# Top-k attention and a tanh-shrink feed-forward on one core: one buffer for turned attention weights, and combined feed-forward weights kept in SBUF

## The chip, the core and the metric

The kernel runs on one NeuronCore of a Trainium2 chip. A core has five engines that run their own instruction queues in order and meet through semaphores: TensorE (PE; its weight loads are listed as PEld), VectorE (DVE), ScalarE (ACT), GpSimd (POOL) and SyncE (SP), which here issues nearly all DMAs. Operands lie in SBUF, matmul results in PSUM, inputs and outputs in HBM. The metric is device time in microseconds of the one core, as the median of the timed runs. Beside these there is one profiled execution, whose trace has every instruction.

## The reference

Attention over 8 batches, 8 heads, 576 tokens and a head size of 64, in which each query keeps its 32 largest scores, and then a feed-forward block over all 4608 tokens of 512 values (8 heads of 64), with 2048 inner values:

```python
scores = scale * np.matmul(q, k.transpose(0, 1, 3, 2))
kth = np.partition(scores, -top_k, axis=-1)[..., -top_k:-top_k + 1]
scores = np.where(scores >= kth, scores, -1000000000.0)
attn = np.exp(scores - np.max(scores, axis=-1, keepdims=True))
attn = attn / (np.sum(attn, axis=-1, keepdims=True) + 1e-09)
x = np.matmul(attn, v)          # heads side by side: 4608 x 512
h = x @ w_in                    # 512 x 2048
g = h - np.tanh(h)
out = g @ w_out                 # 2048 x 512
```

`w_in` and `w_out` arrive as float64 and are turned into float32 on the chip.

## The kernel before

**Attention steps.** Work is cut into 144 steps. A step is one block of 128 queries for a pair of heads (`hp`, four pairs per batch); the 64 remaining queries of a batch form a step of their own for two pairs together (a remainder step, `rem`). A batch from 1 on has 18 steps in two parts: in part 0 the query blocks 0 and 1 of all four pairs, in part 1 blocks 2 and 3, with the remainder steps in part 1 (in part 0 for the last batch). Two steps of the same pair in a part make a group: their turned weights lie side by side and are multiplied with the values at once. The 18 steps of batch 0 turn their weights with matmuls on PE (`pe`).

A step n passes through a row of stages, in successive turns of the main loop in `run`: `scores` (PE, copied by ACT at L338), `search` (DVE finds the 32 largest by `max` and `match_replace`), `mask` (POOL sets the thresholds `tb` at L397, ACT and POOL make `z`), `expo` (ACT), `divide` (ACT, L459), `turn_z` (DVE transposes 32x32 blocks into the single buffer `zx`, L491), `spread_keys` (SP writes `zx` to the DRAM tensor `there`, L507, and one turn later brings it back as the turned weights, L510, four DMAs), and five turns after the step `values` (PE, L558, ten pairs of matmuls for a group). `spread_keys` puts the main groups in turn into two places, `et2[0]` (a tile of its own) and `et2[1]` (the front of `later`, a tile that holds raw weights at the start); remainder steps use a third place, `et_rem`.

**Values.** `load_v` brings a batch's values of a head pair, 2 DMAs of 128 KB, once for each part, into three rotating buffers, and in part 0 the remainder rows too (2 small DMAs).

**Feed-forward.** A full unit is 256 tokens; there are 17 of these (and two of 128 tokens, of batch 0). A full unit has 30 items. Sixteen `ffn_h` items multiply with `w_in` (L609), and every second one makes `g` (tanh and copy on ACT, subtraction on POOL, L623). Then 14 `ffn_p` items multiply with `w_out` by Strassen's scheme in Winograd's form: seven products instead of eight, each in two halves k, with the parts of `g` as A11 to A22 and those of `w_out` as B11 to B22. An item is 8 matmuls of 128x256 (L723). The products are

```python
ORDER = [("A11", "B11"), ("A12", "B21"), ("S2", "T2"), ("S3", "T3"), ("S1", "T1"), ("A22", "T4"), ("S4", "B22")]
```

with S1 = A21 + A22, S2 = S1 - A11, S3 = A21 - A11, S4 = A12 - S2 (`sum_up`, POOL, L695) and T1 = B12 - B11, T2 = B22 - T1, T3 = B12 - B22, T4 = B21 - T2, the combinations of the weights. Those are made once, after the start, by `combine` on POOL (16 instructions, one per item). In the kernel before, T1 replaces B12 and T2 replaces B21 in SBUF; B21, T3 and T4 lie in DRAM (`kept`) and are streamed to SBUF for every unit. `stream` does so on SP (L703): six transfers of 512 KB per unit into two places (`flow`, in the tile `more`), one per half k. Products 1, 3 and 5 use these places one after the other, so the next stream into a place waits until the product that reads it is done. `ffn_p` also evicts the results (ACT, L748 to L765), joins them (POOL, L736) and writes the output (L768).

**Order.** The program's order is fixed by hand. In each turn n of `run` the stages are emitted in a set order, and between them `deal` emits feed-forward items from the list `work`: 0.4 of the turn's share after `search`, and 0.2 at three later places. `rate` sets the share so that the list lasts to the end and units come in time. Each engine then has its instructions in this order, and SP its DMAs: a DMA at the head of SP's queue that waits for a semaphore holds those behind it. What is left in `work` after the last turn is emitted at the end. `due` emits the value matmuls; up to turn 45 it comes first in the turn, from 45 on (`NEAR`) after the second half of the scatter (`coming_back`). At the end the kernel looks whether a step's search was too narrow; only then it runs again with an exact search.

Of the kernel before, what the change touches and what calls it, by code (L numbers as in the profile page):

```python
# [19 lines left out]
J = 4  # L20
# [34 lines left out]
def kernel(  # L55
# [59 lines left out]
    def next_h(name):  # L115
# [16 lines left out]
    zx1 = consts.tile([P, 4 * S], FP32, name="zx")[:]  # L132
    et2 = [consts.tile([P, 4 * S], FP32, name="et")[:], later[:, 0 : 4 * S]]
    et_rem = later[:, 4 * S : 6 * S]

    more = consts.tile([P, 4096], FP32, name="more")[:]
    sums = [
        [more[:, (2 * i + k) * 512 : (2 * i + k + 1) * 512].rearrange("p (m n) -> p m n", n=P) for i in range(2)]
        for k in range(2)
    ]  # L140
    flow = [
        more[:, (2 + k) * 1024 : (3 + k) * 1024].rearrange("p (m n) -> p m n", n=2 * P) for k in range(2)
    ]
    qT0 = [more[:, i * S : (i + 1) * S] for i in range(4)]
# [3 lines left out]
    q_first = more[:, 3264 : 3264 + S]  # L148
    temps = [later[:, i * 512 : (i + 1) * 512].rearrange("p (m n) -> p m n", m=2) for i in range(4)]
    kept = {  # L150
        x: keep.tile([P, CF // 2, 2 * P], FP32, name=f"kept{x}") for x in ("B12", "B21", "T3", "T4")
    }

# [111 lines left out]

    def load_v(b, hp, part):


        if b == 0 and hp == NHP - 1:
            x = vb3  # L270
        else:
            x = kqpool.tile([P, 2, J, D], FP32, tag="vb", name="vb", bufs=3)[:]
        vb[b, hp, part] = x
        y = vrs[hp]
        for t in range(2):
            h, o = 2 * hp + t, t * R
            nc.sync.dma_start(
                x[:, t, :, :], v[b, h, o : o + JP, :].rearrange("(c p) d -> p c d", p=P)
            )
            o = 0 if t else JP  # L280
            if part == 0:
                nc.sync.dma_start(y[half(t), t, :], v[b, h, o : o + R, :])

# [191 lines left out]

    zxs, ets, last_et = {}, {}, [1]

# [18 lines left out]
    def spread_keys(n):  # L496


        zx = zxs.pop(n)
        rem = steps[n].rem  # L500
        if not rem:
            last_et[0] ^= 1
        et = ets[n] = et_rem if rem else et2[last_et[0]]
        assert rem or not last_et[0] or combined[0] == 4 * WJ
        w = steps[n].nq * S // 2
        there = dpool.tile([P, NG * w], FP32, tag=f"there{steps[n].nq}", name="there")
        nc.sync.dma_start(there[:], zx[:, 0 : NG * w])  # L507
        yield
        for c in range(NG):
            nc.sync.dma_start(  # L510
                et[group(c), 0 : NG * w].rearrange("i (a x) -> i a x", a=NG),
                there[:, c * w : (c + 1) * w].rearrange("(a i) x -> i a x", a=NG),
            )

    def turn_pe(n):

        g, z = steps[n], st.pop(n)["z"]
        if g.rem:
            et = et_rem
        elif g.i:  # L520
            et = ets.pop(n - 1)
        else:
            et = et2[0]
        ets[n] = et
        et = tiles(et, g.nq)[:, :, :, g.i, :].rearrange("p a k j -> p k a j")
        for k0 in range(0, KC, J):
            kn = min(J, KC - k0)
            zt = zt_ps.tile([P, 512], FP32, tag="zt", name="zt")
            for k in range(kn):
                nc.tensor.transpose(  # L530
                    zt[:, k * P : (k + 1) * P], z[:, (k0 + k) * P : (k0 + k + 1) * P], ident[:]
                )
            nc.scalar.copy(
                et[:, k0 : k0 + kn],
                zt[:, 0 : kn * P].rearrange("p (k a j) -> p k a j", a=NG, j=G),
            )
            if k0:
                yield
# [5 lines left out]
    def values(n):  # L544
# [7 lines left out]
        for i in range(2 if g.rem else 1):  # L552
# [3 lines left out]
            for c in range(J + 1):  # L556
                for t in range(2):
                    nc.tensor.matmul(  # L558
                        av[half(t), 0, cols],
                        vb[g.b, hp, g.part][:, t, c, :] if c < J else vrs[hp][:, t, :],  # L560
                        es[:, :, (J + 1) * t + c if c < J else J].rearrange("p a i j -> p a (i j)"),
                        start=(c == 0),
                        stop=(c == J),
                    )
# [84 lines left out]

    def keep_corners(j):  # L650

        (_, b12), (b21, _) = corners(w_out[j][:])
        nc.sync.dma_start(kept["B12"][:, 2 * j : 2 * j + 2, :], b12)
        nc.sync.dma_start(kept["B21"][:, 2 * j : 2 * j + 2, :], b21)

    def bring_corners():

        for j in range(WJ):
            (_, b12), (b21, _) = corners(w_out[j][:])
            nc.sync.dma_start(b12, kept["B12"][:, 2 * j : 2 * j + 2, :])  # L660
            nc.sync.dma_start(b21, kept["B21"][:, 2 * j : 2 * j + 2, :])

    def combine(j, x):

        (b11, b12), (b21, b22) = corners(w_out[j][:])
        t3, t2, t4 = (temps[(3 * j + i) % 4] for i in range(3))
        ms = slice(2 * j, 2 * j + 2)
        if x == 0:
            nc.gpsimd.tensor_tensor(t3, b12, b22, ALU.subtract)
            nc.sync.dma_start(kept["T3"][:, ms, :], t3)  # L670
        elif x == 1:
            nc.gpsimd.tensor_tensor(b12, b12, b11, ALU.subtract)
        elif x == 2:
            nc.gpsimd.tensor_tensor(t2, b22, b12, ALU.subtract)
        else:
            nc.gpsimd.tensor_tensor(t4, b21, t2, ALU.subtract)
            nc.sync.dma_start(kept["T4"][:, ms, :], t4)
            nc.sync.dma_start(b21, t2)

# [5 lines left out]
    def sum_up(u, k, x):  # L685

        (a11, a12), (a21, a22) = quarters(u, k)
        s1, s2 = sums[k]
        out_, a, b, op = [
            (s1, a21, a22, ALU.add),  # L690
            (s2, s1, a11, ALU.subtract),
            (a21, a21, a11, ALU.subtract),
            (a12, a12, s2, ALU.subtract),
        ][x]
        nc.gpsimd.tensor_tensor(out_, a, b, op)  # L695

    ORDER = [("A11", "B11"), ("A12", "B21"), ("S2", "T2"), ("S3", "T3"), ("S1", "T1"), ("A22", "T4"), ("S4", "B22")]
    FLOW = ["B21", "T3", "T4"]

    def stream(i):  # L700

        x, k = FLOW[i // 2], i % 2
        nc.sync.dma_start(flow[k], kept[x][:, 4 * k : 4 * k + 4, :])  # L703

    def product(u, i, k):
# [6 lines left out]
        (a11, a12), (a21, a22) = quarters(u, k)  # L712
        lhs = {"A11": a11, "A12": a12, "A22": a22, "S1": sums[k][0], "S2": sums[k][1], "S3": a21, "S4": a12}[left]
        acc = cur[u][i % 2][:, 0 : 2 * P]
        fresh = i in (0, 1, 3)
        for m in range(4):
            if right in FLOW:
                rhs = flow[k][:, m, :]
            else:
                r, c = {"B11": (0, 0), "T1": (0, 1), "T2": (1, 0), "B22": (1, 1)}[right]  # L720
                f = 2 * (4 * k + m) + r
                rhs = w_out[f // FJ][:, f % FJ, c * 2 * P : (c + 1) * 2 * P]
            nc.tensor.matmul(acc, lhs[:, m, :], rhs, start=(fresh and k == 0 and m == 0), stop=(k == 1 and m == 3), skip_group_check=True)  # L723
        return acc

    def ffn_p(u, item):
# [10 lines left out]

        if item in (3, 4):
            sum_up(u, item - 3, 3)
        if item < 3:  # L740
            sum_up(u, 1, item)
        if ORDER[i][1] in FLOW[:-1]:
            stream(2 * FLOW.index(ORDER[i][1]) + 2 + k)
        if not k:
# [24 lines left out]

    combined = [0]  # L770

    def combine_next():

        if combined[0] < 4 * WJ:
            combine(combined[0] // 4, combined[0] % 4)
            combined[0] += 1

    def ffn_small_o(u, part):

        ffn_o(u, 0, part)  # L780
        if u.combines and part:
            combine_next()

    def ffn_full(u, item):

        ffn_h(u, item)
        if item in (6, 7):
            stream(item - 6)
        combine_next()
        if 8 <= item < 11:  # L790
            sum_up(u, 0, item - 8)

# [58 lines left out]
    def run(exact):  # L851
        plan()
        turned_pe[0] = not exact
        combined[0], last_et[0] = 0, 1
        if exact:
# [14 lines left out]
        for n, b, hp, part in sorted(rows):  # L870
            for x, name in enumerate("kq"):
# [12 lines left out]
                else:  # L884
                    at(n - 3 + x, turn)
                    turned[name] = n - 3 + x
            at(n + 3 if b else n - 1, lambda b=b, hp=hp, part=part: load_v(b, hp, part))

# [15 lines left out]
        def part(x, k):  # L904
            next(loaded[k][0])
            if x == 2:
                converted[0] = k + 1
                if k >= WJ * CD and k % CD == CD - 1:
                    keep_corners(k // CD - WJ)
                free.append(loaded[k][1])  # L910
# [74 lines left out]
        for n in range(-4, NS + LAG):  # L985
# [6 lines left out]
            if n < NEAR:  # L992
                due()
            share, usable = rate(), converted[0]
            if pe:
# [9 lines left out]
            if pe:  # L1005
                spread(n - 2)
            deal(0.0 if pe else 0.4)
            for x in coming_back:
                next(x, None)
            coming_back.clear()  # L1010
            if n >= NEAR:
                due()
            if here(1):
# [63 lines left out]
```

## Time and profile before

| | |
|---|---|
| timed runs, us | 1591.86, 1593.54, 1600.24 (median 1593.54) |
| the profiled execution's own time, us | 1588.93 |
| its span, first to last instruction, us | 1587.1 |
| mean granted clock of TensorE | 0.962 |
| DMA traffic on SP's queue | 285.83 MB |
| streams of 512 KB (`more` from `kept`) | 102 |
| scatters of main groups (4 x 288 KB) | 56 |
| value loads of 128 KB into the rotating buffers | 118 |

The page first has each engine's busy time and its share of the span. Other views list groups of instructions by line, operation and tile (count, busy time, mean duration, and the idle time just before them with what ended it); the waits (who waited for what, total, times, longest); busy time by stretch with the granted clock of TensorE; and the timeline, in which a line has start, duration, engine, line of the kernel, operation, tiles (out<-in), count, and in brackets the idle time before it. SPq is SP's queue of DMA issues. `more<-keptT` is a stream of T3 or T4, `more<-keptB` one of B21; `hx` and `hy` are the two PSUM banks of the products; a product that reads a streamed operand is in the row `hy<-more,g`. A wait is put down to the last semaphore seen, so a row can name an engine where a DMA was the cause.

### The profile page before, as it was taken

How to read it: one execution, taken by the hardware profiler on the slowest of the kernel's cores; microseconds unless marked ns; L12 is line 12 of the kernel's file. 1: busy time of each engine (PE TensorE's matmuls, PEld its weight loads, DVE VectorE, ACT ScalarE, POOL GpSimd, SP SyncE). 2: the span in 40 equal slices, each digit the busy share in tenths (PEclk: the TensorE clock that was granted, in tenths of full speed). 3: DMA queues.
4: the chain of work that ended last, by engine and by line, in shares of the span. 5: the costliest groups of instructions: out<-in, count | busy, mean ns of one | idle time of the engine just before them, and what ended most of it. 6: DMA issues, size and time to landing. Idle time of an engine off the chain costs nothing.

```text
span 1587.1 us, 27014 instructions
## 1 busy us (share of the span) xinstructions
PE 1410.6 (89%) x7892; PEld 1069.5 (67%) x7892; DVE 1298.0 (82%) x4914; ACT 1017.1 (64%) x1898; POOL 1105.1 (70%) x1573
## 2 busy tenths in 40 slices
PE   4676997898997989898999899989998988989998
PEld 2464755676665667676777677767676766768887
DVE  7998898998999999898989888989988887873000
ACT  4766766766676767676667666767776665664321
POOL 3777799768585767767587767777777674856523
PEclk9778998999999999999999999999999999999999
DMA  9955126777867977778678886778768776673532
GB/s 262 347 186 195 23 74 172 208 197 192 206 172 200 200 202 195 192 175 216 179 189 201 202 205 180 196 194 202 194 181 207 183 166 174 181 201 112 133 93 69
DMA packets 299292, 287.87 MB, mean 181 GB/s; under 512 B 224384, under 2 KB 234624, under 8 KB 291968
## 3 DMA queue, kind: packets, MB, share of 16 engines
q1 hardware_dynamic: 297360, 285.83, 68.4%
q8 instruction: 65, 1.06, 0.3%
q14 instruction: 91, 0.75, 0.2%
q10 hardware_dynamic: 1776, 0.22, 0.1%
HBM read 196.98 MB, written 87.95 MB: 180 GB/s over the span
## 4 chain that ended last, share of the span: by engine, by line
PE 29%; DVE 26%; DMA 13%; ACT 12%; POOL 12%; issue 5%; SPq 3%; DVEq 0%; ACTq 0%; POOLq 0%
PE hps L609 10%; PE hx L723 6%; PE hy L723 6%; DMA more<-keptT 5%; DVE m L379 4%; DMA there<-zx 4%; DVE top L372 4%; POOL g L623 3%; PE av L558 3%; ACT z L459 3%; ACT z L410 3%; PE scps L330 3%; POOL z L413 3%; DVE zx L491 3%; DVE rest L382 2%
## 5 line engine op out<-in xcount | busy, mean ns | idle before, releaser
L609 PE MATMUL hps<-xT,w_in 128*128 128x256 f32 (+1 forms) x2176 | 478.0, 376 | 13.0 <-ACT g L622 12.0
L413 POOL TENSOR_TENSOR z<-sc,z 128x576 f32<-128x576 f32 x288 | 404.6, 1427 | 79.3 <-ACT z L410 79.3
L609 PEld LDWEIGHTS hps<-xT,w_in 128*128 128x128 f32 x2176 | 394.9, 194 | 93.2 <-issue 23.6
L410 ACT ACTIVATE z<-sc,tb 128x576 f32<-128x576 f32 x288 | 207.6, 768 | 245.1 <-POOL tb L397 241.2
L491 DVE STREAM_TRANSPOSE zx<-z 128x1152 f32<-128x1152 f32 x126 | 172.4, 1368 | 107.8 <-ACT z L459 69.2
L623 POOL TENSOR_TENSOR g<-g,th 128x512 f32<-128x512 f32 x144 | 183.4, 1275 | 97.5 <-ACT g L622 96.7
L723 PE MATMUL hy<-more,g 128*128 128x256 f32 x816 | 208.1, 407 | 37.7 <-DMA more<-keptT 35.2
L433 ACT ACTIVATE z<-z,nb 128x576 f32<-128x576 f32 x288 | 221.8, 776 | 2.4 <-POOL z L413 2.4
L459 ACT ACTIVATE z<-z,rd 128x576 f32<-128x576 f32 x252 | 180.4, 763 | 56.7 <-DVE rd L452 56.5
L723 PEld LDWEIGHTS hy<-more,g 128*128 128x128 f32 x816 | 161.2, 202 | 78.4 <-DMA more<-keptT 20.3
L372 DVE MAX8 top<-ab 128x8 f32<-128x144 f32 x864 | 194.5, 293 | 0.0
L330 PE MATMUL scps<-kT,qT 64*128 64x288 f32 (+1 forms) x1120 | 158.3, 430 | 36.1 <-DVE top L368 34.0
L338 ACT COPY sc<-scps 128x1152 f32<-128x1152 f32 x144 | 160.7, 1116 | 35.8 <-PE scps L330 35.8
L379 DVE MAX8 m<-rest 128x8 f32<-128x168 f32 x576 | 161.1, 321 | 0.0
L443 POOL TENSOR_SCALAR rd<-den 128x2 f32<-128x2 f32 x144 | 32.8, 228 | 182.1 <-ACT z L433 177.8
L379 DVE MAX8 m<-top 128x8 f32<-128x144 f32 (+1 forms) x576 | 151.2, 304 | 0.0
L330 PEld LDWEIGHTS scps<-kT,qT 64*128 64x128 f32 (+1 forms) x1120 | 87.3, 177 | 91.0 <-issue 39.3
L723 PE MATMUL hx<-w_out,g 128*128 128x256 f32 x544 | 133.4, 393 | 16.9 <-POOL g L623 10.0
L723 PEld LDWEIGHTS hx<-w_out,g 128*128 128x128 f32 x544 | 102.9, 194 | 44.2 <-POOL g L623 17.6
L723 PE MATMUL hx<-w_out,more 128*128 128x256 f32 x544 | 127.8, 385 | 0.0
L621 ACT ACTIVATE th<-hps 128x512 f32<-128x512 f32 x144 | 84.4, 586 | 55.3 <-PE hps L609 52.8
L723 PEld LDWEIGHTS hx<-w_out,more 128*128 128x128 f32 x544 | 102.6, 191 | 21.1 <-issue 4.7
(107 smaller groups left out, 2220.5 us busy)
## 6 DMA issues: line engine op xcount, KB each, us to landing
there<-zx SPq DMA_DIRECT2D x56, 1152.0 KB, 5.0
more<-keptT SPq DMA_DIRECT2D x68, 512.0 KB, 5.0
et<-there SPq DMA_DIRECT2D x112, 288.0 KB, 5.6
spare<-there SPq DMA_DIRECT2D x112, 288.0 KB, 6.4
more<-keptB SPq DMA_DIRECT2D x34, 512.0 KB, 6.6
vb<-in_v_dram SPq DMA_DIRECT2D x118, 128.0 KB, 5.3
kin<-in_k_dram SPq DMA_DIRECT2D x116, 72.0 KB, 4.2
out_dram<-ot SPq DMA_DIRECT2D x32, 256.0 KB, 2.3
```

What stands on the lines that cost most here:

```text
L330: nc.tensor.matmul(ps[rows, t, s, 0:S2], qT[g.b, g.hp + i, g.part][half(t), qs], kT[g.b, g.hp + i][half(t), ks], start=True, stop=True,)
L338: nc.scalar.copy(sc[:], ps[:, :, :, 0:S2])
L372: nc.vector.max(top[:, t, o : o + 8], low[:, t, i, :])
L379: nc.vector.max(m[:, t, m8], seen[i][t])
L410: nc.scalar.activation(zv[:, t, :], scf[:, t, :], AF.Relu, bias=tb[:, t : t + 1], scale=-BIG)
L413: nc.gpsimd.tensor_tensor(zv[:, t, :], scf[:, t, :], zv[:, t, :], ALU.subtract)
L433: nc.scalar.activation(x["zv"][:, t, :], x["zv"][:, t, :], AF.Exp, bias=x["nb"][:, t : t + 1], scale=scale, accum_out=den[:, t : t + 1],)
L459: nc.scalar.activation(x, x, AF.Copy, scale=rds[n][:, g.i, t : t + 1])
L491: nc.vector.transpose(tiles(zx, g.nq)[:, :, :, g.i, :].rearrange("p c k j -> p k c j"), z[:].rearrange("p (k c j) -> p k c j", c=NG, j=G),)
L609: nc.tensor.matmul(cur[u][:, s : s + w], w_in[j][:, c, fo : fo + P], u.xT[:, c, 0:w], start=(c == 0), stop=(c == CD - 1),)
L623: nc.gpsimd.tensor_tensor(g, g, th[:], ALU.subtract)
L723: nc.tensor.matmul(acc, lhs[:, m, :], rhs, start=(fresh and k == 0 and m == 0), stop=(k == 1 and m == 3), skip_group_check=True)
```

## The change

Five things are different.

Turned weights: main groups after batch 0 all go to one place, `et_main` (the front of `later`). `et_pe`, the former first place, is used in batch 0 and afterwards holds half of T2 and the sum S1. The `due` of turns from 45 on stands ahead of `coming_back`, so that the value matmuls which read the place precede the scatter which writes it.

Weight combinations: B21 stays where it was in `w_out`. T3 has two places in `more`, T4 has two, T2 has two, of which one (T2's half 0 and T4's half 1) is the same memory. These two halves are also in DRAM, and `bring` fetches them in turn: T4's half at item 4 of a unit's products, T2's half at item 11. `keep_corner` saves only B12 (for the exact run).

Combinations have a new order, and a gate: T3 not before turn 17, T2 and T4 not before turn 20, since their places hold other data until then. The first item of the second small unit may now make one too.

Values: `load_v` runs once per batch and pair; the fourth pair has a place of its own (`vb_last`).

Sums: S2 is written over A11 instead of into a place of its own, so it is made after the A11 product of its half: S1 and S3 of half 0 during `ffn_full`, then S1 of half 1 at item 0, S2 of half 0 and S3 of half 1 at item 1, S2 of half 1 at item 2, S4 at items 3 and 4.

```diff
@@ -130,26 +130,26 @@
     zx1 = consts.tile([P, 4 * S], FP32, name="zx")[:]
-    et2 = [consts.tile([P, 4 * S], FP32, name="et")[:], later[:, 0 : 4 * S]]
+    et_pe, et_main = consts.tile([P, 4 * S], FP32, name="et")[:], later[:, 0 : 4 * S]
     et_rem = later[:, 4 * S : 6 * S]
     more = consts.tile([P, 4096], FP32, name="more")[:]
-    sums = [
-        [more[:, (2 * i + k) * 512 : (2 * i + k + 1) * 512].rearrange("p (m n) -> p m n", n=P) for i in range(2)]
-        for k in range(2)
-    ]
-    flow = [
-        more[:, (2 + k) * 1024 : (3 + k) * 1024].rearrange("p (m n) -> p m n", n=2 * P) for k in range(2)
-    ]
+    whole = {
+        "T3": [more[:, 1024 * i : 1024 * (i + 1)] for i in range(2)],
+        "T4": [more[:, 2048:3072], more[:, 3072:4096]],
+        "T2": [more[:, 3072:4096], et_pe[:, 0:1024]],
+    }
+    whole = {x: [y.rearrange("p (m n) -> p m n", n=2 * P) for y in ys] for x, ys in whole.items()}
+    sums = [et_pe[:, 1024 + 512 * i : 1536 + 512 * i].rearrange("p (m n) -> p m n", n=P) for i in range(2)]
     qT0 = [more[:, i * S : (i + 1) * S] for i in range(4)]
...
     q_first = more[:, 3264 : 3264 + S]
-    temps = [later[:, i * 512 : (i + 1) * 512].rearrange("p (m n) -> p m n", m=2) for i in range(4)]
-    kept = {
-        x: keep.tile([P, CF // 2, 2 * P], FP32, name=f"kept{x}") for x in ("B12", "B21", "T3", "T4")
-    }
+    temps = [later[:, i * 512 : (i + 1) * 512].rearrange("p (m n) -> p m n", m=2) for i in range(2)]
+    vb_last = later[:, 6 * S : 6 * S + 512].rearrange("p (t c d) -> p t c d", t=2, d=D)
+    kept_B12 = keep.tile([P, CF // 2, 2 * P], FP32, name="kept_B12")
+    kept = {x: keep.tile([P, 4, 2 * P], FP32, name=f"kept_{x}") for x in ("T2", "T4")}
     e896 = consts.tile([P, 1], FP32, name="e896")
@@ -263,14 +263,14 @@
             o += r1 - r0
-    def load_v(b, hp, part):
-        if b == 0 and hp == NHP - 1:
-            x = vb3
+    def load_v(b, hp):
+        if hp == NHP - 1:
+            x = vb_last if b else vb3
         else:
             x = kqpool.tile([P, 2, J, D], FP32, tag="vb", name="vb", bufs=3)[:]
-        vb[b, hp, part] = x
+        vb[b, hp] = x
         y = vrs[hp]
@@ -278,8 +278,7 @@
             o = 0 if t else JP
-            if part == 0:
-                nc.sync.dma_start(y[half(t), t, :], v[b, h, o : o + R, :])
+            nc.sync.dma_start(y[half(t), t, :], v[b, h, o : o + R, :])
     turned_pe = [True]
@@ -473,7 +472,7 @@
             )
-    zxs, ets, last_et = {}, {}, [1]
+    zxs, ets = {}, {}
     def group(a):
@@ -498,14 +497,12 @@
         rem = steps[n].rem
-        if not rem:
-            last_et[0] ^= 1
-        et = ets[n] = et_rem if rem else et2[last_et[0]]
-        assert rem or not last_et[0] or combined[0] == 4 * WJ
+        et = ets[n] = et_rem if rem else et_main
         w = steps[n].nq * S // 2
...
         yield
+        assert combined[0] >= 12
         for c in range(NG):
@@ -520,7 +517,7 @@
         else:
-            et = et2[0]
+            et = et_pe
         ets[n] = et
@@ -557,7 +554,7 @@
                         av[half(t), 0, cols],
-                        vb[g.b, hp, g.part][:, t, c, :] if c < J else vrs[hp][:, t, :],
+                        vb[g.b, hp][:, t, c, :] if c < J else vrs[hp][:, t, :],
                         es[:, :, (J + 1) * t + c if c < J else J].rearrange("p a i j -> p a (i j)"),
@@ -647,35 +644,36 @@
         return [[x[:, :, r, c * 2 * P : (c + 1) * 2 * P] for c in range(2)] for r in range(2)]
-    def keep_corners(j):
-        (_, b12), (b21, _) = corners(w_out[j][:])
-        nc.sync.dma_start(kept["B12"][:, 2 * j : 2 * j + 2, :], b12)
-        nc.sync.dma_start(kept["B21"][:, 2 * j : 2 * j + 2, :], b21)
+    def keep_corner(j):
+        nc.sync.dma_start(kept_B12[:, 2 * j : 2 * j + 2, :], corners(w_out[j][:])[0][1])
     def bring_corners():
         for j in range(WJ):
-            (_, b12), (b21, _) = corners(w_out[j][:])
-            nc.sync.dma_start(b12, kept["B12"][:, 2 * j : 2 * j + 2, :])
-            nc.sync.dma_start(b21, kept["B21"][:, 2 * j : 2 * j + 2, :])
-    def combine(j, x):
+            nc.sync.dma_start(corners(w_out[j][:])[0][1], kept_B12[:, 2 * j : 2 * j + 2, :])
+    def combine(x, j):
         (b11, b12), (b21, b22) = corners(w_out[j][:])
-        t3, t2, t4 = (temps[(3 * j + i) % 4] for i in range(3))
-        ms = slice(2 * j, 2 * j + 2)
-        if x == 0:
-            nc.gpsimd.tensor_tensor(t3, b12, b22, ALU.subtract)
-            nc.sync.dma_start(kept["T3"][:, ms, :], t3)
-        elif x == 1:
+        k, ms = j // 2, slice(2 * (j % 2), 2 * (j % 2) + 2)
+        t2 = whole["T2"][k][:, ms, :]
+        if x == "T3":
+            nc.gpsimd.tensor_tensor(whole["T3"][k][:, ms, :], b12, b22, ALU.subtract)
+        elif x == "T1":
             nc.gpsimd.tensor_tensor(b12, b12, b11, ALU.subtract)
-        elif x == 2:
+        elif x == "T2":
             nc.gpsimd.tensor_tensor(t2, b22, b12, ALU.subtract)
+            if k == 0:
+                nc.sync.dma_start(kept["T2"][:, ms, :], t2)
         else:
+            t4 = temps[j % 2] if k else whole["T4"][k][:, ms, :]
             nc.gpsimd.tensor_tensor(t4, b21, t2, ALU.subtract)
-            nc.sync.dma_start(kept["T4"][:, ms, :], t4)
-            nc.sync.dma_start(b21, t2)
+            if k:
+                nc.sync.dma_start(kept["T4"][:, ms, :], t4)
+    COMBINE = [("T3", j) for j in range(WJ)] + [("T1", j) for j in range(WJ)]
+    COMBINE += [(x, j) for j in (2, 3, 0, 1) for x in ("T2", "T4")]
     def quarters(u, k):
@@ -685,22 +683,20 @@
         (a11, a12), (a21, a22) = quarters(u, k)
-        s1, s2 = sums[k]
-        out_, a, b, op = [
-            (s1, a21, a22, ALU.add),
-            (s2, s1, a11, ALU.subtract),
-            (a21, a21, a11, ALU.subtract),
-            (a12, a12, s2, ALU.subtract),
-        ][x]
+        s1 = sums[k]
+        out_, a, b, op = {
+            "S1": (s1, a21, a22, ALU.add),
+            "S3": (a21, a21, a11, ALU.subtract),
+            "S2": (a11, s1, a11, ALU.subtract),
+            "S4": (a12, a12, a11, ALU.subtract),
+        }[x]
         nc.gpsimd.tensor_tensor(out_, a, b, op)
     ORDER = [("A11", "B11"), ("A12", "B21"), ("S2", "T2"), ("S3", "T3"), ("S1", "T1"), ("A22", "T4"), ("S4", "B22")]
-    FLOW = ["B21", "T3", "T4"]
-    def stream(i):
-        x, k = FLOW[i // 2], i % 2
-        nc.sync.dma_start(flow[k], kept[x][:, 4 * k : 4 * k + 4, :])
+    def bring(x):
+        k = 0 if x == "T2" else 1
+        nc.sync.dma_start(whole[x][k], kept[x][:])
     def product(u, i, k):
@@ -710,19 +706,27 @@
         (a11, a12), (a21, a22) = quarters(u, k)
-        lhs = {"A11": a11, "A12": a12, "A22": a22, "S1": sums[k][0], "S2": sums[k][1], "S3": a21, "S4": a12}[left]
+        lhs = {"A11": a11, "A12": a12, "A22": a22, "S1": sums[k], "S2": a11, "S3": a21, "S4": a12}[left]
         acc = cur[u][i % 2][:, 0 : 2 * P]
...
         for m in range(4):
-            if right in FLOW:
-                rhs = flow[k][:, m, :]
+            if right in whole:
+                rhs = whole[right][k][:, m, :]
             else:
-                r, c = {"B11": (0, 0), "T1": (0, 1), "T2": (1, 0), "B22": (1, 1)}[right]
+                r, c = {"B11": (0, 0), "T1": (0, 1), "B21": (1, 0), "B22": (1, 1)}[right]
                 f = 2 * (4 * k + m) + r
...
         return acc
+    SUMS = {
+        0: [(1, "S1")],
+        1: [(0, "S2"), (1, "S3")],
+        2: [(1, "S2")],
+        3: [(0, "S4")],
+        4: [(1, "S4")],
+    }
     def ffn_p(u, item):
@@ -735,12 +739,12 @@
             nc.gpsimd.tensor_tensor(a, a, b, ALU.add)
-        if item in (3, 4):
-            sum_up(u, item - 3, 3)
-        if item < 3:
-            sum_up(u, 1, item)
-        if ORDER[i][1] in FLOW[:-1]:
-            stream(2 * FLOW.index(ORDER[i][1]) + 2 + k)
+        for x in SUMS.get(item, []):
+            sum_up(u, *x)
+        if item == 4:
+            bring("T4")
+        if item == 11:
+            bring("T2")
         if not k:
@@ -767,28 +771,29 @@
                     nc.sync.dma_start(dst, x[rows, :])
-    combined = [0]
+    combined, now = [0], [0]
     def combine_next():
-        if combined[0] < 4 * WJ:
-            combine(combined[0] // 4, combined[0] % 4)
+        if combined[0] < len(COMBINE):
+            x, j = COMBINE[combined[0]]
+            if now[0] < (17 if x == "T3" else 20 if x in ("T2", "T4") else 0):
+                return
+            combine(x, j)
             combined[0] += 1
...
         ffn_o(u, 0, part)
-        if u.combines and part:
+        if u.combines:
             combine_next()
...
         ffn_h(u, item)
-        if item in (6, 7):
-            stream(item - 6)
         combine_next()
-        if 8 <= item < 11:
-            sum_up(u, 0, item - 8)
+        if item in (8, 9):
+            sum_up(u, 0, ("S1", "S3")[item - 8])
     def ffn(u):
@@ -851,7 +856,7 @@
         turned_pe[0] = not exact
-        combined[0], last_et[0] = 0, 1
+        combined[0] = 0
         if exact:
@@ -884,7 +889,8 @@
                     turned[name] = n - 3 + x
-            at(n + 3 if b else n - 1, lambda b=b, hp=hp, part=part: load_v(b, hp, part))
+            if not part:
+                at(n + 3 if b else n - 1, lambda b=b, hp=hp: load_v(b, hp))
@@ -906,7 +912,7 @@
                 if k >= WJ * CD and k % CD == CD - 1:
-                    keep_corners(k // CD - WJ)
+                    keep_corner(k // CD - WJ)
                 free.append(loaded[k][1])
@@ -991,7 +997,7 @@
                 due()
-            share, usable = rate(), converted[0]
+            share, usable, now[0] = rate(), converted[0], n
             if pe:
@@ -1005,11 +1011,11 @@
             deal(0.0 if pe else 0.4)
+            if n >= NEAR:
+                due()
             for x in coming_back:
...
             coming_back.clear()
-            if n >= NEAR:
-                due()
             if here(1):
```

## The prediction

> **What bounds the kernel now.** I read the page's engine sums first, then the busy time by stretch, the waits, and the timeline around one long wait.
>
> ```profile
> span 1587.1 us, 27014 instructions
> PE 1410.6 (89%) x7892; PEld 1069.5 (67%) x7892; DVE 1298.0 (82%) x4914; ACT 1017.1 (64%) x1898; POOL 1105.1 (70%) x1573
> ...
> 250.00:1440.00 1190.00, 1085.88 (x6109) 822.76 (x6109) 1062.62 (x4072) 808.36 (x1500) 859.30 (x1247) 0.97 0.76 192
> 1440.00:1587.10 147.10, 139.74 (x676) 118.25 (x672) 13.14 (x40) 39.79 (x82) 64.71 (x67) 0.99 0.36 105
> ```
>
> The columns of the last two lines are the stretch, its length, busy us of PE, weight loads, DVE, ACT and POOL, the granted clock, DMA share and GB/s. The run has three stages. Up to 250 us weights are converted. From 250 to 1440 the attention steps run with the feed-forward work dealt in between: PE is busy 91% and DVE 89%, so no engine alone is the bound. They hold each other up through in-order queues. From 1440 to the end PE works off what is left, without gaps (0.6 us in all). Only the middle can give much: 104 us without a matmul (1190 - 1086), 127 us without DVE work.
>
> ```profile
> PE hy L723 <- DMA more<-keptT: 35.2, 17, 4.4
> ...
> DVE zx L491 <- DMA there<-zx: 37.5, 14, 6.7
> ...
> SPq L703 <- PE hy L723: 172.6, 39, 29.3
> ...
> SPq L510 <- DMA there<-zx: 61.9, 32, 9.6
> ```
>
> The waits (us in total, times, longest) name the streamed operand: T4, and seldom T3, lands after PE wants it. The chain of waits that ended last gives this transfer 5% of the span, which is the whole flight of some twelve transfers and so more than the idle time behind them. The timeline shows what one late transfer does:
>
> ```profile
> 749.64 2.45 SPq L703 DMA_DIRECT2D more<-keptT  x1
> 756.25 2.74 PE L723 MATMUL hy<-more,g 128*128 128x256 f32 x8 [4.05 <-DMA more<-keptT]
> 758.78 2.87 PE L723 MATMUL hx<-w_out,g 128*128 128x256 f32 x8
> 759.02 0.37 ACT L762 COPY oy<-hy 128x256 f32<-128x256 f32 x1 [6.84 <-PE hy L723]
> 759.47 0.72 POOL L736 TENSOR_TENSOR ot<-ot,oy 128x256 f32<-128x256 f32 x1 [6.43 <-ACT oy L762]
> 760.18 0.59 POOL L397 TENSOR_SCALAR tb<-m 128x1 f32<-128x1 f32 x2
> 763.33 1.38 DVE L491 STREAM_TRANSPOSE zx<-z 128x1152 f32<-128x1152 f32 x1 [1.68 <-ACT z L459]
> ```
>
> PE waits 4.05 us; ACT stands at the eviction of that product, POOL at its join, and the threshold of the next attention step (L397) is queued behind the join. So a stall of PE reaches DVE. After it the eight matmuls take 2.87 us in place of 1.89: the granted clock is halved.
>
> ```profile
> 757.40:760.70 3.30, 3.30 (x9) 2.56 (x9) 3.30 (x20) 0.54 (x2) 1.23 (x3) 0.50 0.28 38
> ```
>
> **Part 1: B21 and T3 are read from SBUF, T4 and T2 share one streamed half.** Each of the 17 full units now issues 6 streams of 512 KB; four must land within four products of the product that frees their place. Afterwards there are two: T4's half, issued at item 4 and read at item 11, and T2's, issued at item 11 and read at item 4 of the next unit, 23 items on. An item takes PE 1.9 us (8 matmuls), so T4 has 7 x 1.9 = 13 us even when items stand back to back, where four had 7.6. Flights of keptT have a median of 5.0 us, of all these streams 10.7 at the longest. I count nothing left of the stall.
>
> What goes: the times without a matmul just before an hy product sum to 37 us after 250 us (nineteen, the largest 4.35, 4.33, 4.05, 3.90 and 3.42). Then the clock. The Trainium skill ("TensorE: Matmul & The Clock Gate", Part 1: The HAM clock gate) says that TensorE falls to half rate after an idle window of about 3.4 us and is back after a busy one. By it the five stalls of 3.4 us and more would cost five windows, 5 x 3.4 / 2 = 8.5 us. The trace has half-clock stretches after eight stalls, of 2.2, 2.4 and 3.0 us too, one of them two windows long: nine windows of 3.41 us, 30.7 us at 0.50, so 15 us lost. The measurement decides: 37 + 15 = 52 us of PE time.
>
> How much of it reaches the end? After the eight longest stalls I took the step with the stall and the next one: 19.4, 20.8, 19.4, 23.3, 21.1, 24.4, 26.7 and 19.7 us, in sum 174.8. Eight times the median of two steps (19.2, by the starts of the score copies L338) is 153.7. So 21 us of the 27.7 + 15 = 42.7 lost there weren't caught up (the step after is often 7.4 us): one half. Half of 52 is **26 us**. Bounds: 10 (DVE and ACT take up most of it) and 52 (nothing was caught up).
>
> **Part 2: fewer transfers.** 68 streams of 524 kB and 56 value loads of 131 kB go: 35.7 + 7.3 = 43 MB of the 285.8 on SP's queue, 15%. Twelve DMAs of the weight combination go too (20 become 8). What could gain are the 37.5 us in which DVE waits for `there` to land. This happens mostly where a remainder step follows and the zx buffer is wanted one step on, with other transfers in flight (flights of 8 to 11 us, against 4.7 alone). I take 15% of it, **5 us**; bounds 0 and 20. SP issues 136 fewer instructions, and its 172.6 us of waiting on PE at the streams shrink with their number; this lies beside other work and isn't counted again. The removed value loads were the second copy of the same values. A batch's head is loaded three steps after its first step, after the last reader of the previous batch in the order of the program, so no wait appears.
>
> **Part 3: one place for turned weights.** The scatter of group m+2 (L510) now writes where the value matmuls (L558) of group m read, and both belong to the same step; the diff puts the matmuls first. I matched each scatter of the trace with the matmuls of the group before. Before 1440 us, 16 of 52 were issued before those matmuls ended, by 0.1 to 3.6 us, 21.8 us in all; the others came later than the matmuls anyway. Behind L510 in SP's queue stand the loads of k, q and v and the next `there`. The Trainium skill ("DMA: Bandwidth & Descriptors", Anatomy of one DMA) speaks against the change: a DMA engine waits on no semaphore, the issuing sequencer does, so each such wait holds all that follows. If each held microsecond were paid, it would be 22 us. The trace has SP held so for 172.6 us at L703, with `there` issued 0.03 us after the transposition in 52 of 70 cases all the same: SP is usually free again when the next `there` is due at the end of the step. The scattered weights themselves lie 5 to 12 us before they are read in those 16 cases, more than the delay. In the tail three scatters are held 2 to 15 us, with 22 to 37 us to spare. I take **-2 us**, bounds 0 and -22.
>
> **Part 4: S2 in A11's place.** The same four sums of 1.27 us for each half. But S2 now waits for the A11 product of its half, queued one product earlier on PE, and is read three items after it is made. The nearest row for the first is S4, which waits in the same way for A12: its 34 instructions have 1.8 us of idle time, 1.3 from PE. For the second the sums' waiters show PE's weight loads 1.8 us behind L695, with more distance than now; at a distance of one item, L623 before the first product has 17.6. I take -2 and -2, **-4 us**, bounds 0 and -20. Queued behind a waiting S2 on POOL are the joins and the next threshold, which is why it counts.
>
> **Part 5: the start.** The 16 combinations stay 16 x 1.27 us on POOL, which is 92% busy from 200 to 250 us, so the order changes but not the sum. Two that ran at 206 and 207 us are held back to a later step by the new gate; what they leave free in front they take behind: **0**, bounds -3 and +3. The first scatter into the main place (264 us) comes some steps after the last combination that uses the same bytes; 0.
>
> **Sum:** 26 + 5 - 2 - 4 = 25 us, from the profiled execution's 1588.9 to 1564. The median of the runs shown, 1593.5, lies 4.6 above it, so **1568 us**. A difference of 0.5% (8 us: below 1585.6, above 1601.5) is about what can be told from no change here.
>
> **The rivals.** *All of it comes back:* with PE's stalls gone ACT and POOL are in time too, and `there` flies faster: 52 + 10 - 4 = 58, 1536 us. For it: the late steps after 1200 us, of 10 to 12 us, have stalls close together. Against: DVE would have to be busy 94% of the middle. *DVE takes it up:* ACT's wait for POOL's threshold (241 us) stays and the catching up was free anyway: 10 + 2 - 4, about 1585 us. *The single place decides, slower:* SP stands at L510 until PE's value matmuls end, `there` comes late, the next transposition waits, and DVE, ACT and PE with it. For it: 52 main groups in the middle, and 14 waits of DVE on `there` already. It cancels the gain when each group costs DVE 0.5 us (25 / 52), and gives +0.5% from 0.65; at 1 us each it is 1568 + 50 = 1618 us. Against it: the covers named in part 3.
>
> **How the numbers follow.** Likeliest 0.56; all of it 0.14; taken up 0.17, half of it within 0.5%; single place 0.13. Faster 0.56 + 0.14 + 0.08 = 0.78, the same 0.09, slower 0.13. The likeliest case's own range is 1553 to 1580 (its half between 0.3 and 0.8). The range from 1543 to 1594 leaves out half of the second case and the slower one.
>
> **What would show it.** Right: no wait of PE on a kept operand above 1 us, 34 streams, hardly a half-clock stretch before hy products, hx and hy matmuls of equal mean (now 407 ns for hy, 385 and 393 for hx), about 243 MB on the queue. Step 3 wrong: SP waits on PE av at L510 by more than 60 us and DVE's wait on `there` grows. Step 4 wrong: L695 idle by more than 10 us on PE, or hx waiting on L695. If PE's idle time before hy is gone and the middle is as long as before, the share of one half was wrong and the stalls were slack.

## The result and the profile after

The changed kernel takes 1556.34 us (median of 4 runs, 1553.7 to 1556.96), the kernel before 1594.1 us (median of 4 runs beside it). The ratio is 0.9754, with a 95% interval of 0.9724 to 0.9784: 2.5% or 39 us less (the two medians are 38 us apart), where the prediction had 25 us and a range that holds the result.

The engine sums of the changed kernel's page:

```profile
span 1555.2 us, 26814 instructions
PE 1404.2 (90%) x7892; PEld 1068.5 (69%) x7892; DVE 1296.3 (83%) x4914; ACT 1015.9 (65%) x1898; POOL 1103.7 (71%) x1573
```

And its busy time by stretch, with the columns as before the change (stretch, length, busy us of PE, weight loads, DVE, ACT and POOL, clock, DMA share, GB/s):

```profile
250.00:1408.00 1158.00, 1079.33 (x6100) 820.11 (x6100) 1061.31 (x4075) 808.58 (x1502) 860.60 (x1248) 0.98 0.64 164
1408.00:1555.20 147.20, 140.35 (x686) 119.17 (x682) 13.91 (x40) 40.33 (x84) 66.74 (x69) 0.99 0.25 73
```

The tail is as long as it was (147 us), and so is the start. The middle lost 32 of the span's 32 us: 1190 became 1158, with the same work in it (DVE 1061 us after 1063). Its DMA share fell from 0.76 to 0.64.

The waits of the changed kernel (us in total, times, longest), of TensorE, DVE and SP. Its lines have moved: L699 is the issue of a streamed operand (L703 before), L503 the write of `there` (L507), L507 the scatter (L510), L693 the sums (L695), L490 the transposition (L491).

```profile
PE scps L329 <- DVE top L367: 35.8, 18, 4.9
...
PE hx L719 <- POOL g L693: 17.4, 12, 3.7
...
DVE zx L490 <- ACT z L458: 86.5, 50, 8.9
DVE scps L359 <- ACT sc L337: 33.1, 35, 3.8
...
SPq L503 <- DVE zx L490: 202.7, 33, 13.1
SPq L699 <- PE hx L719: 96.5, 14, 37.2
...
SPq L507 <- DMA there<-zx: 81.1, 52, 7.0
SPq L507 <- PE av L555: 75.2, 23, 14.0
...
SPq L699 <- PE hy L719: 48.4, 8, 8.9
```

DVE's wait for `z` before the change:

```profile
DVE zx L491 <- ACT z L459: 69.2, 44, 8.9
```

No product waits for a streamed operand any more; the row `hy` on `keptT`, 35.2 us before, is gone. DVE's wait for `there` (37.5 us) fell below the listed rows; in the middle 1.1 us is left. Two rows are new. TensorE waits 17.4 us for POOL's sums (L693), and SP is held 75.2 us at the scatter by the value matmuls (L555). A row has grown: DVE on `z`, from 69.2 to 86.5 us. And SP still waits 96.5 + 48.4 us for products at the streams that are left, though these are a third as many as before (172.6 us at L703).

A count over the middle, from the score copy of step 22 to that of step 143, makes the runs below comparable. Idle of PE is time with neither a matmul nor a weight load, from 60 ns up; the clock's loss is half of the time at a clock of 0.5.

| kernel | middle, us | PE idle | of it before hy | before S2 and S1 products | clock lost | DVE idle | of it on `there` | on `z` | on the score copy |
|---|---|---|---|---|---|---|---|---|---|
| before | 1191.5 | 103.0 | 36.9 | 0 | 30.7 | 123.2 | 37.7 | 51.5 | 33.1 |
| after | 1158.7 | 76.4 | 0.1 | 17.5 | 27.3 | 91.7 | 1.1 | 67.6 | 22.1 |
| streams not waited for | 1152.0 | 77.5 | 0 | 0.8 | 20.5 | 84.5 | 20.7 | 46.8 | 15.7 |
| streams left out | 1148.2 | 69.6 | 0 | 0.8 | 25.6 | 80.7 | 4.3 | 56.1 | 18.7 |
| values loaded once | 1176.0 | 87.9 | 27.3 | 0 | 32.4 | 107.5 | 20.8 | 54.9 | 31.8 |
| one place | 1192.6 | 102.2 | 38.7 | 0 | 34.1 | 124.3 | 30.6 | 53.4 | 37.9 |

Each row is one profiled execution, so a few microseconds of it are chance (that of the values loaded once is 3 us under the median of its runs, that of the one place 5 us above). In every row the middle differs from before by about what DVE's idle time differs. That must be so, since DVE's work is the same in all of them; it shows where the time went, and not by itself what set it free.

### The profile page after: what moved, and what is told of

Its sections match the earlier page's. It is cut to its first block, busy times and chain, and to the rows that moved or that the text cites. A ratio compares the mean times of both kernels' runs of the same rounds, so it can differ in the third digit from the quotient of the medians.

```text
span 1555.2 us, 26814 instructions
## 1 busy us (share of the span) xinstructions
PE 1404.2 (90%) x7892; PEld 1068.5 (69%) x7892; DVE 1296.3 (83%) x4914; ACT 1015.9 (65%) x1898; POOL 1103.7 (71%) x1573
## 3 DMA queue, kind: packets, MB, share of 16 engines
q1 hardware_dynamic: 255248, 239.69, 58.0%
## 4 chain that ended last, share of the span: by engine, by line
PE 30%; DVE 26%; POOL 16%; ACT 16%; issue 5%; DMA 5%; SPq 0%; DVEq 0%; ACTq 0%; POOLq 0%
PE hps L606 11%; PE hx L719 6%; PE hy L719 6%; DVE m L378 4%; POOL g L620 4%; ACT z L458 4%; DVE top L371 4%; ACT z L409 4%; POOL z L412 4%; POOL g L693 3%; PE av L555 3%; PE scps L329 3%; DVE zx L490 3%; ACT z L432 3%; DVE rest L381 3%
## 5 line engine op out<-in xcount | busy, mean ns | idle before, releaser
L490 DVE STREAM_TRANSPOSE zx<-z 128x1152 f32<-128x1152 f32 x126 | 172.0, 1365 | 88.6 <-ACT z L458 86.5
L329 PE MATMUL scps<-kT,qT 64*128 64x288 f32 (+1 forms) x1120 | 161.6, 439 | 42.4 <-DVE top L367 35.6
L337 ACT COPY sc<-scps 128x1152 f32<-128x1152 f32 x144 | 160.7, 1116 | 21.2 <-PE scps L329 20.8
L442 POOL TENSOR_SCALAR rd<-den 128x2 f32<-128x2 f32 x144 | 32.7, 227 | 171.4 <-ACT z L432 165.0
L719 PE MATMUL hy<-more,g 128*128 128x256 f32 x544 | 130.0, 391 | 0.1
L719 PEld LDWEIGHTS hy<-more,g 128*128 128x128 f32 x544 | 105.1, 196 | 21.7 <-issue 4.6
L365 DVE TENSOR_TENSOR ab<-scps,sc 128x576 f32<-128x576 f32 x144 | 107.4, 746 | 0.0
L555 PE MATMUL av<-spare,vb 128*64 128x256 f32 (+1 forms) x1056 | 97.4, 327 | 0.0
## 6 DMA issues: line engine op xcount, KB each, us to landing
there<-zx SPq DMA_DIRECT2D x56, 1152.0 KB, 4.7
```

The costliest lines, as they stand in the source:

```text
L329: nc.tensor.matmul(ps[rows, t, s, 0:S2], qT[g.b, g.hp + i, g.part][half(t), qs], kT[g.b, g.hp + i][half(t), ks], start=True, stop=True,)
L337: nc.scalar.copy(sc[:], ps[:, :, :, 0:S2])
L490: nc.vector.transpose(tiles(zx, g.nq)[:, :, :, g.i, :].rearrange("p c k j -> p k c j"), z[:].rearrange("p (k c j) -> p k c j", c=NG, j=G),)
```

## The experiments

Three theories were set against each other. In the stall theory, that of the prediction, the gain comes from TensorE no longer waiting for streams. In the traffic theory it comes from a lighter DMA queue. In the place theory the single place holds the scatters back and so keeps them out of the way of `there`. The kernel before stands beside all four runs on one chip, with a median of 1588.39 us (19 runs). The microseconds behind a ratio are worked out from the ratio; where the two medians give another figure, it stands beside.

### Streams that nobody waits for

```diff
+    scratch = [keep.tile([P, 4, 2 * P], FP32, name=f"scratch{i}") for i in range(6)]
+    streams = [0]
     def stream(i):
         x, k = FLOW[i // 2], i % 2
-        nc.sync.dma_start(flow[k], kept[x][:, 4 * k : 4 * k + 4, :])
+        streams[0] += 1
+        dst = flow[k] if streams[0] <= 6 else scratch[i][:]
+        nc.sync.dma_start(dst, kept[x][:, 4 * k : 4 * k + 4, :])
```

> The kernel before, in which only the first full unit has its six operands streamed into SBUF; for the other sixteen units the same six transfers of 512 KB go from DRAM to a DRAM scratch that nobody reads, so that the number of DMAs and the bytes read stay, but no product of TensorE waits for them and SP does not wait for the products. Left out: the products with B21, T3 and T4 use the first unit's T4 from the second unit on. Stall theory (half of 52 us of TensorE time comes back): 26 us faster, 18 to 35; the waits of hy on kept operands gone, DVE's wait for the transfer of turned weights still 25 to 38 us. Traffic theory (the gain comes from a lighter DMA queue): 0 to 8 us faster, since the transfers stay. Place theory (holding the scatter back keeps it out of the way of the write): as the traffic theory.

Measured: 1552.34 us, ratio 0.9759 (0.9722 to 0.9796), 38 us faster (36 by the medians). The row of SP's queue on the page:

```profile
q1 hardware_dynamic: 297360, 285.83, 68.7%
```

DVE's waits:

```profile
DVE zx L491 <- ACT z L459: 64.3, 43, 8.9
DVE scps L360 <- ACT sc L338: 26.8, 36, 3.1
DVE zx L491 <- DMA there<-zx: 20.7, 12, 4.1
```

The queue carries as many packets and bytes as before (285.83 MB), and the gain is there all the same. The traffic theory's 0 to 8 us falls. The stall theory holds, but its 26 us was too little; the 35 at the top of its range lies just below the measured value and within the interval (32 to 44 us). Two effects are in this run and it can't part them: TensorE doesn't wait for the streams, and SP isn't held by the products (172.6 us of waiting at L703 before). The second may be what shows in DVE's wait for `there`, which fell from 37.5 to 20.7 us with the same bytes in the queue (the transfers now end in DRAM instead of SBUF, which may help as well).

### Streams left out

```diff
+    streams = [0]
     def stream(i):
         x, k = FLOW[i // 2], i % 2
-        nc.sync.dma_start(flow[k], kept[x][:, 4 * k : 4 * k + 4, :])
+        streams[0] += 1
+        if streams[0] <= 6:
+            nc.sync.dma_start(flow[k], kept[x][:, 4 * k : 4 * k + 4, :])
```

> The kernel before, in which the six streams are left out from the second full unit on (96 transfers of 512 KB fewer, 50 MB of 286). Left out: the products with B21, T3 and T4 use what the first unit left there. Stall theory: as the kernel without the wait, 26 to 32 us faster, at most 6 us faster than that one, DVE's wait for the transfer of turned weights 20 to 35 us. Traffic theory: 15 us or more faster than the kernel without the wait, and DVE's wait for the transfer of turned weights below 8 us.

Measured: 1546.07 us, ratio 0.9707 (0.9669 to 0.9745), 46 us faster (42 by the medians). DVE's waits in this run:

```profile
DVE zx L491 <- ACT z L459: 73.7, 52, 8.9
DVE scps L360 <- ACT sc L338: 31.1, 39, 3.1
...
DVE zx L491 <- DMA there<-zx: 4.2, 2, 3.2
```

Taking 50 MB off the queue brings 6 us more than taking the waits away (1552.3 to 1546.1; the four runs of each don't overlap, though the intervals of the two ratios do, and the middles of the two profiles lie 3.8 us apart). So the traffic as such, with the time that SP takes to issue it, is worth about a seventh of this gain. The traffic theory's 15 us or more for this step falls. It was right on its other number, DVE's wait for `there`, which is nearly gone; the stall theory's 20 to 35 us for that was wrong, and so were its 26 to 32 us for the whole. Of the 16 us that left this wait, 9 came back as a wait for `z` on the same instruction. DVE's transposition needs both its input `z` from ACT and a free `zx`; when one comes earlier, the other is the last.

### Values loaded once

```diff
+    vb_last = later[:, 6 * S : 6 * S + 512].rearrange("p (t c d) -> p t c d", t=2, d=D)
...
-    def load_v(b, hp, part):
-        if b == 0 and hp == NHP - 1:
-            x = vb3
+    def load_v(b, hp):
+        if hp == NHP - 1:
+            x = vb_last if b else vb3
...
-            at(n + 3 if b else n - 1, lambda b=b, hp=hp, part=part: load_v(b, hp, part))
+            if not part:
+                at(n + 3 if b else n - 1, lambda b=b, hp=hp: load_v(b, hp))
```

> The kernel before with the values of a batch loaded once instead of once for each part (56 loads of 128 KB fewer, 7.3 MB), with the fourth pair's own place. Stall theory: 0 to 2 us faster. Traffic theory: a sixth of the 43 MB that the whole change takes away, so 4 to 8 us faster, with DVE's wait for the transfer of turned weights lower by 5 to 12 us.

Measured: 1578.79 us (10 runs), ratio 0.9943 (0.992 to 0.9966), 9 us faster. Waits of TensorE and DVE:

```profile
PE hy L723 <- DMA more<-keptT: 25.2, 11, 3.8
...
DVE zx L491 <- DMA there<-zx: 20.8, 12, 4.0
```

That is more than the stall theory gave it (0 to 2). It is a little over the top of the traffic theory's 4 to 8, and the measured interval, 5 to 13 us, takes in part of that range; DVE's wait fell by 16.7 us, where that theory had 5 to 12. 56 loads of 128 KB are only 7.3 MB, a seventh as much as the streams of the run before. The rows show two ways in which they cost: the streams' own stalls fell from 35.2 to 25.2 us, and DVE's wait for `there` from 37.5 to 20.8. A value load is 131 kB in pieces of 256 bytes, and its issue held SP up to 2.59 us in the trace of before (at 1115.9 us). So these loads stood in SP's queue or in the DMA engines ahead of transfers that were waited for. Both show in the traces, for the fourteen writes of `there` that belong to remainder steps: the time from the transposition to SP's issue fell from 18.6 to 9.4 us in sum, and the median flight from 8.8 to 7.7 us. No run has one without the other.

### One place for the turned weights

```diff
-        if not rem:
-            last_et[0] ^= 1
-        et = ets[n] = et_rem if rem else et2[last_et[0]]
-        assert rem or not last_et[0] or combined[0] == 4 * WJ
+        et = ets[n] = et_rem if rem else et2[0]
...
+            if n >= NEAR:
+                due()
             for x in coming_back:
                 next(x, None)
             coming_back.clear()
-            if n >= NEAR:
-                due()
```

> The kernel before with one place for the turned weights of main groups, the value matmuls put before the scatter in the order of the program; all else as before. Stall theory: 2 us slower, 0 to 10, because SP is held at the scatter by 20 to 40 us in the middle. Place theory: 5 to 20 us faster, with shorter flights of the transfer of turned weights in front of remainder steps, and DVE's wait for it at 20 us or less.

Measured: 1588.45 us (10 runs), ratio 0.9987 (0.9964 to 1.001): no difference, at most 6 us faster and 2 slower. SP's waits in this run:

```profile
SPq L700 <- PE hy L720: 133.9, 38, 29.2
SPq L507 <- DMA there<-zx: 60.6, 32, 9.7
SPq L507 <- PE av L555: 55.9, 22, 14.9
```

SP is held 55.9 us at the scatter, 40.9 of them in the middle (foreseen were 20 to 40), and it costs nothing that can be told. The place theory, with 5 to 20 us of gain, falls on the time, and DVE's wait for `there` only fell to 30.4 us, not to 20. The stall theory's 2 us loss lies at the edge of the interval, and most of its range (0 to 10) outside. Part of the hold is not new: SP waits 133.9 us at the streams in place of 172.6.

## Why the prediction was right, point by point

**Part 1, the streams.** The mechanism was right: nothing waits for an operand from `kept`, no half-clock stretch follows an hy product, and hy and hx products have means of 391 and 396 ns. The stall of 37 us is gone whole. The clock's 15 us are not: over the middle its loss fell by 3.4 us, from 30.7 to 27.3, because half-clock stretches now follow other pauses. Two of them come after waits for S2, from 814.6 and 1193.4 us.

The 26 us were too few for a part that, taken alone with all its waits, measured 36 to 38. In that run the 36.9 us before hy are gone and the clock's loss fell from 30.7 to 20.5 us, 47 us of TensorE's time together. If all 38 are put down to these, the share that came back is four fifths and not one half. But DVE's wait on `there`, which the prediction left out of this part, is 17 us less in the same run; taken off, it leaves 21 us for the stalls, and one half would stand. So either the half was wrong, or it was wrong to count nothing for what else the streams hold up. Which of the two stays open, since no run took the one without the other.

The prediction also let SP's waits at the streams shrink with their number. They shrank by a quarter, though the streams became a third: in the middle SP waits 43.6 + 24.6 us for products at the streams, where it waited 90.0 us before. With 59.5 us at the scatter that is 128 us, more than before. DVE's wait on `there` went all the same, so the sum of SP's waits doesn't tell what they cost.

**Part 2, the transfers.** The count was right (34 streams, 239.69 MB on the queue; foreseen were 243). The size wasn't: 15% of the 37.5 us was taken, and 36.6 of 37.7 us in the middle went. One reading was wrong as well. The flights of 8 to 11 us are not those of a group whose write stands before a remainder step; they are mostly the remainder steps' own writes, half as large. The rows of these writes before and after the change (times issued, KB, median us to landing):

```profile
there<-zx SPq DMA_DIRECT2D x14, 576.0 KB, 8.8
...
there<-zx SPq DMA_DIRECT2D x14, 576.0 KB, 7.1
```

In the trace before, 11 of the 14 waits of DVE on `there`, 32.7 of 37.5 us, ended with such a write. DVE wants the buffer again mostly 7 to 8 us after the transposition, so what counts is how late SP issues the write, and how long it flies. Both over all six traces (the sum over the fourteen writes of the time from the transposition's end to the issue, their median flight, and DVE's wait in the middle, us):

| kernel | issued late | flight | DVE's wait on `there` |
|---|---|---|---|
| before | 18.6 | 8.8 | 37.7 |
| after | 6.8 | 7.1 | 1.1 |
| streams not waited for | 9.1 | 8.3 | 20.7 |
| streams left out | 5.7 | 5.7 | 4.3 |
| values loaded once | 9.4 | 7.7 | 20.8 |
| one place | 20.0 | 8.5 | 30.6 |

A small cut in the two takes away nearly the whole wait. But it doesn't pay in full. `z` became the last input (51.5 to 67.6 us).

**Part 3, the single place.** Right as far as the runs can tell. The sign that was named against it, over 60 us of SP at the scatter, did appear (75.2 us with the tail, 59.5 in the middle). Its second half, a growing wait on `there`, did not. The rule of the Trainium skill ("DMA: Bandwidth & Descriptors", Anatomy of one DMA, written for GpSimd's path) that a semaphore wait happens on the issuing sequencer fits SP in this trace, by these 75.2 us. It doesn't say whether such a wait costs anything: alone, with SP held 55.9 us, this part moved the kernel by nothing that can be told (ratio 0.9987, 0.9964 to 1.001). The covers that the prediction read from the trace were enough.

**Part 4, S2 in A11's place.** Half of it failed. POOL doesn't wait for the A11 product (the sums have 3.8 us of idle time in all, foreseen were 2 more than 1.8). But the other 2 us, for TensorE waiting on S2, is 17.4 us: this step failed, and its sign named by the prediction, hx waiting on the sums, appeared. The groups of matmuls by operand show where, in S2's two halves:

```profile
L719 PE MATMUL hx<-et,g 128*128 128x256 f32 x136 | 34.4, 397 | 9.7 <-POOL g L693 9.7
L719 PE MATMUL hx<-more,g 128*128 128x256 f32 x136 | 33.1, 386 | 7.8 <-POOL g L693 7.8
```

And the timeline around the longest of these waits shows why:

```profile
806.07 1.27 POOL L693 TENSOR_TENSOR g<-g 128x512 f32<-128x512 f32 x1
807.33 0.58 POOL L396 TENSOR_SCALAR tb<-m 128x1 f32<-128x1 f32 x2
807.48 1.99 PE L719 MATMUL hx<-more,g 128*128 128x256 f32 x8
...
808.53 2.77 POOL L412 TENSOR_TENSOR z<-sc,z 128x576 f32<-128x576 f32 x2 [0.41 <-ACT z L409]
...
811.28 0.63 POOL L416 TENSOR_SCALAR bad<-top,tb 128x3 uint8<-128x3 f32 x2
811.87 1.28 POOL L693 TENSOR_TENSOR g<-et,g 128x512 f32<-128x512 f32 x1
...
813.20 2.49 PE L719 MATMUL hx<-et,g 128*128 128x256 f32 x8 [3.73 <-POOL g L693]
```

S2 of half 1 belongs to item 2. It stands in POOL's queue behind the next step's threshold work (L396 to L416, 807.3 to 811.9 us), and TensorE, which is ahead of POOL, comes to item 5 first. The prediction took the rows of the old sums, which are read after more items, and had put 17.6 us as the case of a neighbour at one item's distance; that upper bound was nearly what came. A cure to try would be to ask for S2 one item earlier, ahead of the threshold work. Neither that nor this part alone was run, so what the 17.4 us cost in the end stays open. The middle is 10.5 us longer than in the run without streams, which has 0.8 us there; that points to S2, but the two kernels differ in more than this.

**Part 5, the start,** was right: the copy of step 22 starts at 252.1 us, before at 250.3.

**The sum.** Parts 1 and 2 were 31 us. The run with nearly all streams left out measured 42 to 46, and the value loads alone 9; the changed kernel gained 38 to 39. What lies between isn't taken apart: it keeps 34 streams, it pays for S2, and the gains needn't add up. The direction and the mechanism were foreseen and the size was not: the saving was put 13 to 14 us too low, and it was the width of the range that held the result. No rival came true as told: the single place cost nothing that can be told, DVE's other waits took back only a part, and of the 58 us of the best case 39 came.

## What to carry to other kernels

Count a late transfer's stall on the engine that waits, and then also what stands behind it in its issuing queue: here most of the streams' cost went when nothing waited for them any more and they waited for nothing, and only about a seventh more when their bytes went too. The length of a queue's waits is no measure of their cost; look for the transfer that is issued late and wanted soon. When a wait goes, ask which input of the same instruction is next; DVE's 36 us on `there` came back by 16 us on `z`. A value that is made in place of another, later than before, must be looked for in the queue of the engine that makes it: what counts is which long work stands between its turn and the reader, not the number of items.

## What the runs showed of the hardware

Large transfers took longer or shorter without a plain relation to the bytes in the queue. The 1152 KB write of `there` has a median of 5.0 us before and 4.7 in the changed kernel, which moves 16% fewer bytes on the queue (285.83 to 239.69 MB). But with the streams left out (235.50 MB) it stayed at 5.0, and with the values loaded once (278.49 MB) it was 4.7. The 576 KB write of the remainder steps, smaller and yet slower, fell most with the streams left out, from 8.8 to 5.7 us. Leaving out 56 loads of 128 KB alone took DVE's wait for `there` from 37.5 to 20.8 us.

The half clock came after short pauses too. In the changed kernel pauses of TensorE of 1.84 us (at 1374.8 us) and 2.47 us (at 1104.7) were each followed, within 3.5 us, by 3.41 us at a clock of 0.5, while others of 1.5 to 1.9 us were not. What separates them is found by counting on the grid on which the half-clock stretches of a trace begin, a step of 3.413 us. The step around the pause at 1104.7 us, with a matmul in 0.95 of its 3.41 us, and the next one, at a clock of 0.50:

```profile
1104.70:1108.11 3.41, 0.95 (x4) 0.87 (x5) 3.38 (x10) 3.41 (x9) 2.32 (x3) 1.00 0.94 239
1108.11:1111.52 3.41, 3.41 (x9) 2.66 (x8) 3.41 (x15) 0.67 (x3) 3.10 (x5) 0.50 0.92 144
```

Over the middles of all six traces there are 1955 such steps at full clock (matmul ends as the profile models them). Each of the 75 in which TensorE had no matmul for 1.96 us or more in sum was followed by a step at 0.5; of the 1873 with less than 1.87 us none was; of the seven between, two were, the one at 1374.8 among them. So a pause can be short and count, or long and not: one of 3.52 us (streams not waited for, at 1102.9 us) fell into two steps, with 1.73 and 1.79 us without a matmul, and the clock stayed full. The Trainium skill ("TensorE: Matmul & The Clock Gate", Part 1: The HAM clock gate) names an idle window of about 3.4 us that runs free of the work; the length fits these traces, but somewhat more than half a window without matmuls was enough here.
